# A tile's transposes asked for one projection later, with four row buffers, and staged weight blocks made on GpSimd

## The chip, the cores and the metric

The kernel runs on one core of one Trainium2 chip. The metric is the device time of one execution in microseconds (us). The kernel before was timed three times; a profiled execution, one more, gives the trace on which the reading rests. Engine names: PE is the matrix engine (PEld its weight loads), DVE the vector engine, ACT the scalar engine, POOL is GpSimd, SP is the sync engine, which here only issues transfers (DMAs).

## The reference

A transformer block in float32 with 2048 rows and 640 columns: attention in a window of 256 with 32 heads of width 20, and a gated network whose gate mixes the rows.

```
h  = x  + attention(layernorm(x), wqkv) @ wo
z  = gelu(layernorm(h) @ w_in)              # 640 -> 1728
z1, z2 = z[:, :864], layernorm(z[:, 864:])
g  = w_sp @ z2 + b_sp                       # 2048 x 2048 times 2048 x 864
out = h + (z1 * g) @ w_out                  # 864 -> 640
```

## The kernel before, in words

A tile is 128 of the 2048 rows; there are NT = 16. Products in full precision are made of pieces: a number is split into a high part (a copy on ACT, L719, into the matrix engine's rounded format) and a low part (a subtract on DVE, L713), and high x high, high x low and low x high are summed. The products of the gated network pair two tiles and use seven products of half blocks for eight (the blocks are called B11, T1, T2, B22, T3, B21, T4); sums and differences of blocks are made on DVE and sometimes POOL.

In time order the kernel runs: the dense q, k, v product and attention (to about 460 us); the output projection; the z stage (first half of w_in's columns and part of the second); the z2 stage (layer norm of the second half); the first gate; three more z2 pairs; the second gate with the last product.

**The output projection** is a loop over 16 tiles. For tile i it loads and normalises attention's output, runs 30 matmuls (L94) into a PSUM bank wo_ps, adds the residual on DVE, and forms a layer norm: squares on ACT (L1247), small steps on DVE (L1249, L1251) and POOL (L1250), then the normalised row hn(i) on ACT (L1252). The memory of hn(i) alternates between two places in the buffer m1. The function turn_h(i) transposes hn(i) on PE, five 128 x 128 blocks (L838), copies them to a buffer ho on ACT, and stores them to hn_d in DRAM by SP (L840). In the program, turn_h(i-2) stands behind projection i, and the last two tiles' turns stand in the first two steps of the z stage.

**The z stage** works on pairs of tiles, z_pair(q). It loads two tiles of hn_d into the buffer fx (L871, L872), copies and subtracts them into the operand buffer aw, and then runs eight products (L898) per pair in steps. A list `steps` holds the products; `at(n, f)` puts a piece of work f ahead of step n (a negative n is an iteration of the projection's loop, counted from its end).

**The z2 stage and the gate.** z2_pair(8..15) forms the second half of z for two tiles (L950) and normalises it, in row buffers (rows[0..3]). The gate (first_gate, then second_gate) multiplies pieces of w_sp, loaded into fx (L1036), with blocks of z2: zl and ze. The eighth group's blocks have no room at this point, so z2_pair(12) is "ahead": its seven blocks are formed in the rows on DVE, stored to z2_d (L992), and then read back one by one into the buffer `stage` (SP, L1011), split there on ACT and DVE, and stored to zp_d with high and low part (SP, L1014). They are loaded into ze once room is there (L1015). The same memory `stage` receives a piece of w_out later (L1193), also on SP. Results of the first gate are stored to g_d from the row buffers (L1099, L1100).

**What sets the order.** Up to the end of attention the order is written by hand. From the projection on, a scheduler orders each engine's instructions by its own simulation of their times; the program's order, and so `at`, only feeds it. Every engine, and SP's and POOL's queue of DMAs with it, runs its instructions in the order it got them.

Of the kernel before, what the change touches and what calls it, by code (L numbers as in the profile page):

```python
# [7 lines left out]
F32 = mybir.dt.float32  # L8
# [26 lines left out]
def block_kernel(ctx, tc, x, wqk, wv, wo, w_in, wsp, bsp, w_out, out):  # L35
# [22 lines left out]
    z2_d = dram.tile([7, P, HF], F32, name="z2_d")  # L58
# [71 lines left out]
    def m1(lo, *shape):  # L130
        return view(mem["m1"], lo, *shape)
# [629 lines left out]
    def hn(i):  # L761
        return m1((4 + i % 2) * D, D)
# [91 lines left out]
    def z_pair(q, i, j, w):  # L854
# [27 lines left out]
        at(n0 - 5, lambda: (plus(s1, a21, a22), copy(part[T1][0], s1), minus(a21, a11, a21)))  # L882
        at(n0 - 4, lambda: (minus(a11, s1, a11), minus(a12, a12, a11), copy(ah[:, 640:1152], ri[:, :512])))
# [47 lines left out]
    def z2_pair(q, i, j, k, ahead=False):  # L931
# [54 lines left out]
        if ahead:  # L986
            at(n0 + 2, lambda: (stat(0, 1), norm(0)))
            at(n0 + 4, lambda: (stat(1, 1), norm(1)))
            b11, b12, b21, b22 = blocks
# [5 lines left out]
            at(n0 + 5, lambda: (keep(B21, b21), keep(B22, b22)))  # L995
            at(n0 + 7, lambda: (minus(b11, b12, b11), minus(b12, b22, b12)))
            at(n0 + 8, lambda: (keep(T1, b11), keep(T3, b12)))
            at(n0 + 9, lambda: minus(b11, b22, b11))
            at(n0 + 10, lambda: (keep(T2, b11), minus(b21, b21, b11)))
            at(n0 + 11, lambda: keep(T4, b21))  # L1000
# [6 lines left out]
    def staged_pieces(n0, n1):  # L1007
        raw = stage.bitcast(F32)[:, 1]
# [199 lines left out]
    staged_pieces(len(steps) + 8, len(steps) + 49)  # L1208
# [15 lines left out]
    for i in range(NT):  # L1224
# [14 lines left out]
        if i > 1:  # L1239
            turn_h(i - 2)  # L1240
# [18 lines left out]
    for n in range(len(steps)):  # L1259
        run(n)  # L1260
        if n < 2:
            turn_h(NT - 2 + n)
# [43 lines left out]
```

## Time and profile before

| | us |
|---|---|
| median of three runs | 1127.86 |
| lowest, highest | 1126.88, 1131.13 |
| the profiled execution | 1126.43 |
| its span in the trace | 1124.6 |
| PE busy in the span | 1090.6 |
| DVE, ACT, POOL busy | 719.1, 576.7, 307.4 |

Rows of the trace are read as follows. A timeline row has its start and duration in us, the engine, the line, the operation, and the tiles it writes and reads; a bracket gives the time the engine stood idle ahead of it, and what ended that. A row of waits gives who waited for whom, the us in all, the number of times and the longest. A row of a stretch gives the busy time of each engine between two moments. PEclk is the clock granted to PE, 1.00 being full speed.

### The profile page before, as it was taken

The page shows a single profiled execution, that of the slowest core. Times are in us where ns is not written, and L with a number is a line of the kernel's source. Part 1 is how long each engine was busy: PE and PEld are TensorE (multiplying, and loading weights), DVE is VectorE, ACT ScalarE, POOL GpSimd, SP SyncE. Part 2 cuts the span into 40 slices and gives each one's busy share as a digit, 9 for nine tenths or more (in the row PEclk, how much of TensorE's full clock was granted, in tenths as well). Part 3 has the DMA queues.
Part 4 walks back from the last instruction along what each step waited for, and adds up shares of the span by engine and source line. Part 5 has one row for each costly group of instructions (what it writes and reads, how often), then busy time and mean ns, then how long its engine had stood idle before and what let it go on. Part 6 is the DMA issues. An engine that isn't in the chain of part 4 may idle for free.

```text
span 1124.6 us, 27720 instructions
## 1 busy us (share of the span) xinstructions
PE 1090.6 (97%) x10667; PEld 976.9 (87%) x10667; DVE 719.1 (64%) x2049; ACT 576.7 (51%) x1228; POOL 307.4 (27%) x454
## 2 busy tenths in 40 slices
PE   8999999999999999989899999999999999999998
PEld 7998877668888776879899999889989899999998
DVE  6541113889999997687376578555547884556442
ACT  4334333259999999566666567333336521222210
POOL 3114444457777778311100254000002000000000
PEclk9999999999999999999999999999999999999999
DMA  7212665656666653688564511654371563344331
GB/s 258 77 31 100 174 213 175 207 199 200 205 214 205 203 166 122 199 277 271 208 194 161 166 54 40 200 179 166 124 256 40 177 211 118 125 148 147 99 95 59
DMA packets 88036, 181.78 MB, mean 162 GB/s; under 512 B 11536, under 2 KB 49680, under 8 KB 83984
## 3 DMA queue, kind: packets, MB, share of 16 engines
q1 hardware_dynamic: 85600, 174.76, 48.2%
q10 hardware_dynamic: 2304, 5.24, 1.2%
q8 instruction: 84, 1.38, 0.5%
q14 instruction: 48, 0.39, 0.1%
HBM read 118.65 MB, written 62.51 MB: 161 GB/s over the span
## 4 chain that ended last, share of the span: by engine, by line
PE 71%; DMA 9%; DVE 7%; issue 4%; POOL 3%; ACT 3%; SPq 2%; POOLq 0%; ACTq 0%; DVEq 0%
PE g L1086 18%; PE out_ps L1125 8%; PE pv L431 6%; PE bank L403 5%; PE bank L337 5%; PE zb L950 4%; PE zx L898 3%; PE zv L898 2%; PE qk L521 2%; PE qk L523 2%; PE qk L522 2%; DMA fx<-hn_d 2%; PE zy L898 2%; POOL sg L540 2%; DMA fx<-wsp_in 1%
## 5 line engine op out<-in xcount | busy, mean ns | idle before, releaser
L406 ACT ACTIVATE pt<-bank 128x384 f32<-128x384 f32 (+2 forms) x512 | 200.3, 492 | 11.8 <-PE bank L403 8.1
L719 ACT ACTIVATE aw<-fx 128x512 fp32r<-128x512 f32 (+2 forms) x160 | 93.0, 594 | 158.9 <-PE g L1086 91.0
L1086 PE MATMUL g<-zl,aw 128*128 128x432 f32 x768 | 171.9, 359 | 1.3 <-ACT zl L719 1.2
L349 DVE CUSTOM_DVE_ANT_0 junk<-bank,strip 128x288 bf16<-128x288 f32 x392 | 157.6, 454 | 2.6 <-PE bank L337 1.1
L1086 PEld LDWEIGHTS g<-zl,aw 128*128 128x128 f32 x768 | 143.6, 188 | 8.7 <-ACT zl L719 1.9
L1086 PE MATMUL g<-ze,aw 128*128 128x432 f32 x576 | 135.8, 363 | 6.0 <-DVE row L713 4.2
L431 PE MATMUL pv<-pt,v_sb 128*32 128x192 f32 (+3 forms) x1984 | 126.5, 321 | 2.5 <-POOL pt L411 1.8
L1086 PEld LDWEIGHTS g<-ze,aw 128*128 128x128 f32 x576 | 106.3, 188 | 14.6 <-ACT aw L719 5.5
L713 DVE TENSOR_TENSOR aw<-fx,aw 128x512 fp32r<-128x512 f32 (+2 forms) x152 | 96.9, 646 | 27.7 <-ACT aw L719 26.0
L403 PE MATMUL bank<-slot 123*32 123x288 bf16 (+5 forms) x1536 | 105.9, 280 | 3.1 <-issue 2.2
L1125 PE MATMUL out_ps<-wout,y_sp 128*128 128x320 f32 (+1 forms) x630 | 96.5, 309 | 0.4 <-ACT y_sp L135 0.4
L408 POOL TENSOR_SCALAR_AFFINE_SELECT pt<-pt 128x512 f32<-128x512 f32 x128 | 82.7, 647 | 47.1 <-ACT pt L406 46.1
L950 PE MATMUL zb<-win,aw 128*128 128x432 f32 x480 | 95.5, 359 | 0.0
L1125 PEld LDWEIGHTS out_ps<-wout,y_sp 128*128 128x128 f32 (+1 forms) x630 | 94.3, 188 | 1.2 <-ACT y_sp L135 0.7
L950 PEld LDWEIGHTS zb<-win,aw 128*128 128x128 f32 x480 | 89.9, 188 | 4.9 <-DVE aw L713 0.4
L337 PE MATMUL bank<-slot 120*32 120x288 bf16 (+2 forms) x1264 | 89.0, 283 | 1.1 <-DVE mcol L349 1.0
L537 DVE TENSOR_TENSOR rest<-qk,sg 128x512 f32<-128x512 f32 x40 | 27.7, 691 | 86.2 <-ACT sg L535 82.0
L411 POOL TENSOR_SCALAR_AFFINE_SELECT pt<-pt 128x512 f32<-128x512 f32 x112 | 73.7, 658 | 0.0
L713 POOL TENSOR_TENSOR aw<-fx,aw 128x640 fp32r<-128x640 f32 x8 | 13.5, 1692 | 217.2 <-ACT aw L719 217.2
L403 PEld LDWEIGHTS <-slot 123*32 123x32 bf16 x1536 | 52.7, 96 | 18.3 <-issue 7.4
L431 PEld LDWEIGHTS pv<-pt,v_sb 128*32 128x32 f32 x1984 | 59.5, 110 | 7.5 <-POOL pt L411 3.8
L540 POOL TENSOR_TENSOR sg<-rest,sg 128x512 bf16<-128x512 f32 x40 | 46.6, 1166 | 69.2 <-ACT sg L539 63.5
(193 smaller groups left out, 2172.7 us busy)
## 6 DMA issues: line engine op xcount, KB each, us to landing
fx<-wsp_in SPq DMA_DIRECT2D x32, 512.0 KB
slot<-qk_d SPq DMA_DIRECT2D x72, 200.0 KB
qk_d<-sg SPq DMA_DIRECT2D x32, 384.0 KB
slot<-qk_d SPq DMA_DIRECT2D x72, 160.0 KB
fx<-hn_d SPq DMA_DIRECT2D x32, 320.0 KB
o_d<-ot SPq DMA_DIRECT2D x64, 128.0 KB
z_d<-row SPq DMA_DIRECT2D x16, 432.0 KB
g_d<-row SPq DMA_DIRECT2D x16, 432.0 KB
```

The source lines that it names most:

```text
L337: nc.tensor.matmul(ps[32 * j:32 * j + 32, :n], part(st, half, 120, 0, hh, q0, 32), part(st, half, 120, 1, hh, lo + skip * j, n), start=Tru ...
L349: nc.vector.tensor_tensor_reduce(out=junk[:, :n], in0=ps[:, :n], in1=keep, scale=1.0, scalar=NEG, op0=OP.add, op1=OP.max, accum_out=m_cols ...
L403: nc.tensor.matmul(ps[32 * i:32 * i + 32, b:e], part(st, half, 123, 1, hh, k0, 32), part(st, half, 123, 0, hh, kb * P + b, e - b), start=T ...
L406: nc.scalar.activation(pt[:, hh, :n], ps[:, :n], AF.Exp, scale=SCALE)
L408: nc.gpsimd.affine_select(out=pt[:, :, :P], in_=pt[:, :, :P], pattern=[[0, 4], [1, P]], base=0, channel_multiplier=-1, compare_op=OP.is_ge ...
L431: nc.tensor.matmul(ps[32 * hh:32 * hh + 32, a - 512 * c:b - 512 * c], v_sb[:, kb, v0:v0 + 32], pt[:, hh, a - kb * P:b - kb * P], start=fir ...
L713: (eng or nc.vector).tensor_tensor(out=out, in0=a, in1=b, op=op)
L719: nc.scalar.activation(out, a, AF.Copy)
L898: nc.tensor.matmul(ps, a[x], b[:, y], start=start and m + x + y == 0, stop=stop and m == n - 1 and x == 1, skip_group_check=True)
L950: nc.tensor.matmul(b[0][:, :HF], a[t][:, x, kk], win2[0][:, y, kk, h * HF:(h + 1) * HF], start=kk + x + y == 0, stop=kk == KD - 1 and x == 1)
L1086: nc.tensor.matmul(ps, w[m][x][:, k], zc[k][m][:, y], start=start and k + x + y == 0, stop=stop and k == 3 and x == 1, skip_group_check=True)
L1125: nc.tensor.matmul(ps[j][:, :HD], src[:w, a, k, :], e1["wout"][:w, b, k, j * HD:(j + 1) * HD], start=(k == 0 and a + b == 0), stop=(k == K ...
```

## The change

There are two parts. The first touches the end of the output projection: hn(i) gets four places in turn (two in m1, two more in fx, and for tiles 14 and 15 the row buffers 2 and 3), turn_h(i-3) stands behind projection i and the last three turns in the z steps 0 to 2, and the first z pairs load and prepare their tiles later (pair 0 loads at the loop's iteration 11 and pair 1 at iteration 15; their first preparations move to the loop's last three or four iterations). The second part gives the staged blocks to GpSimd: z2_pair(12) stores its two normalised rows whole, and staged_pieces loads the pieces, subtracts where a block is a difference, splits and stores, with all of it, DMAs included, on POOL; two intermediate blocks go through a scratch tensor t_d.

```diff
     def hn(i):
-        return m1((4 + i % 2) * D, D)
+        if i % 4 < 2:
+            return m1((4 + i % 2) * D, D)
+        return rows[i % 4][:, :D] if i > 11 else view(fx, (i % 4 - 2 + i // 9 * 2) * D, D)
...
     def turn_h(i):
-        if i < NT - 2:
+        if i < NT - 3:
...
-        at(max(n0 - 13, -10), load)
-        at(n0 - 7, lambda: copy(ah[:, :640], ri))
-        at(n0 - 6, lambda: lo(ah[:, :640], al[:, :640], ri))
+        at(max(n0 - 13, 4 * q - 5), load)
+        at(max(n0 - 7, -4), lambda: copy(ah[:, :640], ri))
+        at(max(n0 - 6, -3), lambda: lo(ah[:, :640], al[:, :640], ri))
...
         if ahead:
-            def keep(m, raw):
-                nc.sync.dma_start(z2_d[m], raw)
-            at(n0 + 4, lambda: keep(B11, b11))
...
-            at(n0 + 11, lambda: keep(T4, b21))
+            for t in range(2):
+                at(n0 + 4 + t, lambda t=t: nc.sync.dma_start(z2_d[t], z[t]))
...
     def staged_pieces(n0, n1):
+        hi, raw = (stage.bitcast(F32)[:, k] for k in range(2))
+        eng = nc.gpsimd
+        def piece(m, src, less=None, keep=None):
+            eng.dma_start(raw, src)
+            if less is not None:
+                eng.dma_start(hi, less)
+                minus(raw, raw, hi, eng)
+            if keep is not None:
+                eng.dma_start(keep, raw)
+            eng.tensor_copy(out=stage[:, 0], in_=raw)
+            minus(stage[:, 1], raw, hi, eng)
+            eng.dma_start(zp_d[m], stage.bitcast(F32))
+        for i, p in enumerate(((B11, b11), (T1, b12, b11, t_d[0]), (B21, b21), (T2, b22, t_d[0], t_d[1]), (B22, b22),
+                               (T3, b22, b12), (T4, b21, t_d[1]))):
+            at(n0 + 6 * i, lambda p=p: piece(*p))
...
-            n = n0 + 6 * i
-            at(n, lambda m=m: nc.sync.dma_start(raw, z2_d[m]))
-            at(n + 2, lambda: copy(stage[:, 0], raw))
-            at(n + 3, lambda: minus(stage[:, 1], raw, stage[:, 0].bitcast(F32)))
-            at(n + 4, lambda m=m: nc.sync.dma_start(zp_d[m], stage.bitcast(F32)))
...
-    staged_pieces(len(steps) + 8, len(steps) + 49)
+    staged_pieces(len(steps) + 4, len(steps) + 49)
...
-        if i > 1:
-            turn_h(i - 2)
+        if i > 2:
+            turn_h(i - 3)
...
-        if n < 2:
-            turn_h(NT - 2 + n)
+        if n < 3:
+            turn_h(NT - 3 + n)
```

The order on PE at the end of the projection and the start of the z stage, before (wo_ps15 is the last tile's projection; ht_psN, or ht_aN with ht_bN, the transposes of tile N; zv0, zx0, zy0 products of the first z pair):

```order
L94 MATMUL wo_ps15_10411<-xb1_98,xb0_97 128x320 x2
L838 MATMUL ht_ps11_10338<-ident_75,m1_8947 128x128 x5
L94 MATMUL wo_ps15_10411<-xb0_97 128x320 x2
L838 MATMUL ht_ps12_10393<-ident_75,m1_8947 128x128 x5
L838 MATMUL ht_ps13_10442<-ident_75,m1_8947 128x128 x5
L898 MATMUL zv0_10465<-zl2_9595,aw_9615 128x432 x3
L898 MATMUL zv0_10465<-zl3_9596,aw_9615 128x432 x3
L838 MATMUL ht_a14_10473<-ident_75,m1_8947 128x128 x4
L838 MATMUL ht_b14_10474<-ident_75,m1_8947 128x128
L898 MATMUL zx0_10486<-zl0_9593,aw_9615 128x432 x3
```

The same place now (lines are numbered 3 higher there, and at L95 by 1; the transposes of tile 11 stand further up, behind seven of the last projection's 30 products):

```order
L95 MATMUL wo_ps15_10404<-xb0_98 128x320 x2
L841 MATMUL ht_ps12_10435<-ident_76,m1_8948 128x128 x5
L901 MATMUL zv0_10458<-zl2_9596,aw_9616 128x432 x3
L901 MATMUL zv0_10458<-zl3_9597,aw_9616 128x432 x3
L841 MATMUL ht_a13_10466<-ident_76,m1_8948 128x128 x4
L841 MATMUL ht_b13_10467<-ident_76,m1_8948 128x128
L901 MATMUL zx0_10479<-zl0_9594,aw_9616 128x432 x3
L901 MATMUL zx0_10479<-zl1_9595,aw_9616 128x432 x3
L841 MATMUL ht_a14_10487<-ident_76,row2_9612 128x128 x4
```

Three sets of transposes stood between the last two products of the projection and the first of z; now one does, and tile 13's come after six z products.

POOL's order where the staged blocks begin, before (mvz are small steps of z2's layer norm, aw operands of the gate and of z):

```order
L976 TENSOR_TENSOR mvz11_1_11633<-mvz11_1_11633,half_78 128x1
L976 TENSOR_TENSOR mvz12_0_11692<-mvz12_0_11692,half_78 128x1
L976 TENSOR_TENSOR mvz12_1_11738<-mvz12_1_11738,half_78 128x1
L713 TENSOR_TENSOR aw_9615<-fx_9616,aw_9615 128x640 x2
L976 TENSOR_TENSOR mvz13_0_12752<-mvz13_0_12752,half_78 128x1
```

And now, the first block and the beginning of the second:

```order
L979 TENSOR_TENSOR mvz12_1_11741<-mvz12_1_11741,half_79 128x1
L1006 DMA stage_9614<-z2_d_73 128x432
L1012 CAST stage_9614<-stage_9614 128x432
L714 TENSOR_TENSOR stage_9614<-stage_9614 128x432
L1014 DMA zp_d_75<-stage_9614 128x864
L1006 DMA stage_9614<-z2_d_73 128x432
L1008 DMA stage_9614<-z2_d_73 128x432
L714 TENSOR_TENSOR stage_9614<-stage_9614 128x432
L1011 DMA t_d_74<-stage_9614 128x432
L1012 CAST stage_9614<-stage_9614 128x432
```

Where POOL had nothing to do between two z2 pairs, it now has 38 instructions, 20 of them DMAs.

SP's order in the first gate, before, from the third pair's store on (row buffers to g_d are the gate's results, fx from wsp_in the weights of a later pair, stage from w_out_in the load into the staged memory):

```order
L1014 DMA zp_d_74<-stage_9613 128x864
L1099 DMA g_d_71<-row2_9611 128x864
L1193 DMA stage_9613<-w_out_in 128x640
L1036 DMA fx_9616<-wsp_in 128x1024
L1100 DMA g_d_71<-row3_9612 128x864
L1036 DMA fx_9616<-wsp_in 128x1024
L1099 DMA g_d_71<-row0_9609 128x864
L1036 DMA fx_9616<-wsp_in 128x1024
```

Now, from two pairs later on:

```order
L1105 DMA g_d_71<-row3_9613 128x864
L1041 DMA fx_9617<-wsp_in 128x1024
L1104 DMA g_d_71<-row2_9612 128x864
L1198 DMA stage_9614<-w_out_in 128x640
L1041 DMA fx_9617<-wsp_in 128x1024
L1105 DMA g_d_71<-row1_9611 128x864
L1041 DMA fx_9617<-wsp_in 128x1024
L1104 DMA g_d_71<-row0_9610 128x864
L1020 DMA ze0_10526<-zp_d_75 128x864
```

The staged blocks' loads and stores are gone from SP's queue, and the load of w_out into their memory has moved from the third pair's store of g (the row buffer 2, 760.54 us in the trace) to the fifth's (794.33 us).

More of the change, by code (lines that the diff above doesn't have):

```diff
@@ L57, in block_kernel @@
     wo_d = dram.tile([KD, P, D], F32, name="wo_d")
-    z2_d = dram.tile([7, P, HF], F32, name="z2_d")
+    z2_d = dram.tile([2, P, FH], F32, name="z2_d")
+    t_d = dram.tile([2, P, HF], F32, name="t_d")
     zp_d = dram.tile([7, P, 2, HF], F32, name="zp_d")
@@ L877, in lo @@
             minus(l, raw, h.bitcast(F32))
[L879 to L883 removed]
+        at(max(n0 - 13, 4 * q - 5), load)
+        at(max(n0 - 7, -4), lambda: copy(ah[:, :640], ri))
+        at(max(n0 - 6, -3), lambda: lo(ah[:, :640], al[:, :640], ri))
+        at(max(n0 - 5, -3), lambda: (plus(s1, a21, a22), copy(part[T1][0], s1), minus(a21, a11, a21)))
+        at(max(n0 - 4, -3), lambda: (minus(a11, s1, a11), minus(a12, a12, a11), copy(ah[:, 640:1152], ri[:, :512])))
         at(n0 - 3, lambda: lo(*part[T1], s1))
```

8 lines of the change are left out of this document (1 added, 7 removed).

## The prediction

> **What bounds the kernel now.** I read the page's busy times first, then a table of stretches, then what TensorE waits for in the two stretches that the change touches, then the chain that ended last.
>
> ```profile
> PE 1090.6 (97%) x10667; PEld 976.9 (87%) x10667; DVE 719.1 (64%) x2049; ACT 576.7 (51%) x1228; POOL 307.4 (27%) x454
> ```
>
> TensorE is busy for 97% of the span, so a change that leaves the matmuls alone can only bring back idle time of PE. The table by stretches (start and end, length, then busy us of PE, PEld, DVE, ACT, POOL, the granted clock, the DMA share, GB/s) tells where that lies.
>
> ```profile
> 460.00:546.00 86.00, 79.11 (x549) 77.32 (x548) 61.82 (x149) 50.42 (x91) 8.66 (x14) 0.98 0.83 276
> 546.00:556.00 10.00, 6.96 (x37) 6.13 (x36) 2.02 (x10) 7.76 (x15) 1.65 (x3) 0.83 0.35 134
> 556.00:640.00 84.00, 84.00 (x433) 80.46 (x432) 51.88 (x104) 52.23 (x96) 1.60 (x1) 1.00 0.52 171
> 640.00:709.00 69.00, 69.00 (x352) 65.72 (x351) 53.68 (x103) 46.41 (x80) 33.67 (x29) 1.00 0.23 71
> 709.00:762.00 53.00, 48.40 (x240) 43.98 (x239) 30.20 (x52) 18.56 (x37) 0.00 (x0) 1.00 0.54 187
> 762.00:838.00 76.00, 74.91 (x380) 70.88 (x379) 39.13 (x63) 28.18 (x51) 0.00 (x0) 1.00 0.53 170
> ```
>
> The output projection and the step into the z stage (460 to 556) lose 86.00 - 79.11 + 10.00 - 6.96 = 9.9 us; the z and z2 products lose nothing; the first gate loses 53.00 - 48.40 = 4.6 us up to 762 and 1.1 after it. The waits of PE from 430 to 560 us, and its timeline around the end of the projection, name the first loss (time in all, times, longest; then start, duration, and in brackets the idle time before the row).
>
> ```profile
> PE ht_ps L838 <- ACT m L1252: 7.8, 5, 2.5
> PE wo_ps L94 <- DVE xb L173: 1.6, 1, 1.6
> PE ht_ps L838 <- ACT ho L719: 0.5, 1, 0.5
> ```
>
> ```profile
> 495.40 0.76 PE L838 MATMUL ht_ps<-ident,m 128*128 128x128 f32 x5 [2.38 <-ACT m L1252]
> 550.88 1.10 PE L838 MATMUL ht_ps<-ident,m 128*128 128x128 f32 x5 [2.54 <-ACT m L1252]
> 551.64 2.51 PE L898 MATMUL zv<-zl,aw 128*128 128x432 f32 x6
> 560.06 1.33 PE L898 MATMUL zx<-zl,aw 128*128 128x432 f32 x6
> ```
>
> Of the 9.9 us, 7.8 are transposes that stand on PE before ACT has written the normalised row (L1252). Idle time costs twice: six products at 551.64 take 2.51 us, and six like them at 560.06 take 1.33, so the pause is followed by 1.2 us of slow clock. The other pause has its own:
>
> ```profile
> 495.00:500.00 5.00, 4.60 (x22) 4.60 (x23) 3.52 (x10) 2.92 (x6) 1.06 (x1) 0.66 0.98 382
> 500.00:521.00 21.00, 21.00 (x148) 20.73 (x146) 18.66 (x48) 15.48 (x32) 2.31 (x4) 1.00 0.90 308
> ```
>
> A granted clock of 0.66 over 5 us is 5 x 0.34 = 1.7 us. In the 21 us after it PE is never idle, though DVE is busy for 18.66 and the DMA engines at 0.90: those two are near a limit, but are not the limit.
>
> In the gate, the waits from 709 to 762 us and the chain read as follows.
>
> ```profile
> PE g L1086 <- DVE row L713: 3.5, 3, 1.9
> PE g L1086 <- ACT aw L719: 1.1, 1, 1.1
> ```
>
> ```profile
> ACT stage L719 <- DMA stage<-z_d: 20.5, 6, 4.8
> DVE stage L713 <- ACT stage L719: 12.2, 5, 3.2
> ```
>
> ```profile
> 704.67 4.35 DMA z_d<-row
> 709.04 2.69 DMA stage<-z_d
> 712.98 2.41 DMA zp_d<-stage
> ...
> 753.85 2.40 DMA zp_d<-stage
> 756.26 2.42 DMA stage<-z_d
> 760.66 66.30 PE g L1086 x336
> ```
>
> ACT and DVE, which feed the gate, stand 20.5 and 12.2 us behind the staged blocks' loads, and PE stands 3.5 + 1.1 = 4.6 us behind them. From 760.66, when the staged work is over, PE runs 336 products without a break. So what each half of the change can win has a ceiling: about 11 to 13 us in the projection, with the clock, and 4.6 to 5.7 in the gate.
>
> **Part 1: the projection.** The program asks for turn(i-3) in place of turn(i-2), but the scheduler had already put the transposes four to five projections behind and now pulls the last ones forward: the transposes of tiles 11, 12 and 13, which stood inside and behind the last projection, become 11 inside it, 12 behind it, and 13, 14, 15 among the first z products. What makes this free is the number of buffers, four normalised rows in place of two: ACT need no longer wait for a turn before it writes the next row, and PE meets a row that has long been written. I take the whole 7.8 + 0.5 us as gone, with the 1.7 us of clock at 495: 10.0 us. The 1.6 us behind DVE xb (L173) stays. z starts at 551.64 - 10.0 = 541.6 us.
>
> What is late next: four of the added rows lie where the z stage's first tiles are to be loaded. Loads of tiles were issued (chain rows: start, duration) at
>
> ```profile
> 483.54 7.23 DMA fx<-hn_d
> 512.52 5.81 DMA fx<-hn_d
> 523.97 6.55 DMA fx<-hn_d
> ```
>
> 483 to 524 us before, well ahead. Now the load of tile 2 waits for turn 10 and that of tile 3 for turn 11, which stands behind the seventh of the last projection's 30 products. 25 products take 3.67 us, so the 23 left take 3.4, that load issues near 538, and it lands after the 5.81 to 7.23 us of the rows: at 544 to 545.
>
> ```profile
> 538.36 3.67 PE wo_ps L94 x25
> ```
>
> ACT's copy from tile 3 and DVE's subtract stand in their queues ahead of the sum and the row of tile 15 and ahead of evacuations of the first z products. PE has some 26 products of 0.196 us (1.17 for six, chain row below) and two sets of transposes in hand, about 6 us, so it runs out near 547, when the ACT and DVE work behind the load is under way.
>
> ```profile
> 554.97 1.17 PE zx L898 x6
> ```
>
> The stall lies between nothing (the load lands at 544 and the copies are quick) and 7.2 us (a whole load). I take 3.0, since the load lands ahead of 547 but three or four ACT and DVE steps of 0.6 to 0.9 us follow it; the 1.2 us of clock then stays as it is. The first part is 10.0 - 3.0 = 7.0 us faster, 3 to 10 with its bounds.
>
> SP's queue is moved too: behind the loads of tiles 0 to 3 stand loads of later tiles and win1's pieces. They come 10 to 50 us later than before, when the queue had room (DMA share 0.35 from 546, 0.52 from 556), so I cost that at nothing beyond the stall.
>
> **Part 2: the staged blocks on GpSimd.** ACT loses seven copies and DVE eleven subtracts (7 here, 4 that stood in the z2 rows):
>
> ```profile
> L719 ACT ACTIVATE stage<-stage x7: 562/564/567, 711.7 to 758.8; 128x432 fp32r<-128x432 f32 x7
> L713 DVE TENSOR_TENSOR stage<-stage x7: 596/607/610, 712.3 to 759.4; 128x432 fp32r<-128x432 f32 x7
> ```
>
> 7 x 0.564 = 3.9 us and 11 x 0.607 = 6.7 us: off the path by themselves, but with them go the waits of 20.5 and 12.2 us in those queues, and so PE's 4.6 us. Against it stands sharing between DVE and POOL:
>
> ```profile
> L713 DVE TENSOR_TENSOR aw<-fx,aw 128x512 fp32r<-128x512 f32 x3 | 2.8, 917 | 0.4 <-ACT aw L719 0.4
> ```
>
> ```profile
> L713 DVE TENSOR_TENSOR aw<-fx,aw 128x512 fp32r<-128x512 f32 x39 | 26.4, 686 | 10.5 <-ACT aw L719 10.4
> ```
>
> 917 ns in 640 to 700 us, where POOL is about half busy, against 686 in the gate, where it is not used. The z2 stretch, where this happens, still has PE busy 69.00 of 69.00 us, and DVE in the gate is busy 30.20 of 53. I leave 0.6 us for it: 4.0 us faster, from 2.5 to 5.7.
>
> POOL takes over a serial chain: per block a load, a cast, a subtract and a store, with four more loads and subtracts. The trace has no DMA issued by GpSimd and no cast there. The subtract is known:
>
> ```profile
> L713 POOL TENSOR_TENSOR row<-row,row 128x432 f32<-128x432 f32 x6 | 8.1, 1344 | 7.2 <-DVE row L713 3.4 <-ACT row L982 1.5 <-DVE zl L713 1.1
> ```
>
> 11 x 1.34 = 14.7 us; seven casts between ACT's 0.56 and 1.34, taken as 0.85: 6.0; four second loads at 0.7 us of issue each (estimate): 2.8. That is 23.5 us beside 14 transfers in series of L each. L is at least the 2.4 to 2.7 of SP's rows above; a factor of two is the far end. I take 3.2, nearest to those rows: 14 x 3.2 + 23.5 = 68 us, from 709 to 777. With L = 2.6 it ends at 769, with 5.2 at 805. The Trainium skill ("DMA: Bandwidth & Descriptors", Anatomy of one DMA, the gpsimd path) gives 2.0 us plus size over 436 GB/s, by which 216 KB take 2.5 and 432 KB 3.0 us; by it the chain would end near 771 (an estimate), and no run so far shows it.
>
> Who waits for the chain: only the load of w_out into the same stage memory, on SP, now behind the store of g that came fifth after 762.50, and behind it in the queue the wsp load that came next.
>
> ```profile
> 762.50 0.33 SPq L1193 DMA_DIRECT2D stage<-w_out_in  x1
> ...
> 794.33 0.33 SPq L1099 DMA_DIRECT2D g_d<-row  x1
> 797.58 0.33 SPq L1036 DMA_DIRECT2D fx<-wsp_in  x1
> ```
>
> In before's clock that wait becomes due at 794 and hurts from 797.6. Seen from a gate that runs earlier by 7.0 in start and 4.0 in work, the chain starts earlier by 7.0 as well, so only the 4.0 count: it must end by 793. At 777 it has 16 us to spare. The blocks themselves are wanted after 838.
>
> Sum: 7.0 + 4.0 = 11.0 us. The profiled execution took 1126.43 us (span 1124.6), 1.4 below the median of the three runs: 1115.4 on its scale, 1116.9 on the median's; I write 1117.0.
>
> **The rivals.** First, slower: GpSimd's chain outlasts its deadline and SP stands behind the w_out load, with wsp loads and stores of g behind it. It decides from 793, so from L = (793 - 709 - 23.5) / 14 = 4.3 us. PE cannot run ahead of a wsp load by more than one pair, so what is late beyond it is lost almost one to one. With L at 6.3 (POOL's issue held up behind DVE work besides the transfer, 3.7 above SP's rows) it ends at 821, 28 late: 7.0 and 4.0 won, 28 lost, 1127.9 + 17 = 1145; at L = 5.2, 12 late, about 1129. For it speaks that POOL shares something with DVE (686 to 917 ns) and is slower at each step (1344 against 607); against it that DVE is idle for over 40% of the gate. The Trainium skill ("SBUF — State Buffer", SBUF: two separate sides) states a rule that speaks for it: the shared port pair is held for a whole instruction, and a GpSimd-issued DMA of 620 ns took about 3100 beside a DVE copy. The longer DVE rows agree with sharing; whether issues suffer, no row here shows. I give this rival 0.13, of which 0.09 is slower by over 0.5%.
>
> Second, the opening of z gives most of the first gain back. If tile 3's load takes 7 us and pairs 0 and 1 are prepared behind it, now that their preparation has moved from 505 to 530 us into the opening, PE stands 7 us and more: 10.0 - 7.5 + 4.0 = 6.5, so 1121.4, and with a second pause at pair 2 about 1124. For it: the last 10 us of the projection have a DMA share still high.
>
> ```profile
> 536.00:546.00 10.00, 10.00 (x73) 9.99 (x72) 2.92 (x13) 6.64 (x12) 1.65 (x3) 1.00 0.87 314
> ```
>
> Against it: DVE has only 2.92 and ACT 6.64 us of work in these 10, so the preparations fit. Chance 0.20.
>
> Third, the projection does not get shorter by 10.0, as the pauses were hiding DVE (18.66 of 21 us busy) and the transfers (0.83 of the time over 86 us). Were DMA at 0.95 the limit, 86 us could only become 86 x 0.83 / 0.95 = 75, so it does not bind; DVE's slack does not forbid it either, but one late add costs 1 to 2 us. A gain of 5 there less 3 is 2, with the gate's 4: 1122. Chance 0.10. That the change does not do what it says is the case where rows still come late to PE, in its own right 0.04: only the gate's 4.0 is left less the stall of 3.0, near 1127.
>
> **How the numbers follow.** The forecast has 0.53; the rivals 0.13, 0.20, 0.10 and 0.04. Half a per cent, 5.6 us, is about what a measurement of this kernel can tell from no change, so faster means below 1122.2 and slower above 1133.5. Faster: all of the forecast (0.53), two thirds of the second (0.13), half of the third (0.05), a little of the first: 0.72. Slower: 0.09. Same: 0.19. The forecast's own bounds are 10.0 + 5.7 = 15.7 and 3 + 2.5 = 5.5 us, so 1112 to 1122; the low end goes to 1110 for the clock that an opening without a pause would keep (1.2), the high end to 1127, which holds the second and third rivals.
>
> **What would show it.** Right: no wait of ht_ps behind ACT m of more than 0.5 us, clock 1.00 through 495 to 500, z's first product near 541.6; one or two PE waits of together about 3 us within 10 us of it, ended by ACT or DVE that stand behind a load of hn_d; in the gate no ACT or DVE wait for stage and PE waits under 1 us; POOL's last store of zp_d near 766 to 775 by the clock of after, ahead of the w_out load. Wrong: POOL DMAs of over 4.3 us in mean, a gap of PE near 790 behind wsp loads, gaps of over 6 us at z's opening, or a projection that ends after 546.

## The result, and the profile after

The changed kernel's median is 1119.49 us (six runs, 1116.56 to 1122.58) against 1129.0 for the kernel before (six runs, 1126.88 to 1131.13). The ratio is 0.9928 with an interval of 0.9903 to 0.9953: 8.1 us less, between 5.3 and 11.0. The forecast was 11.0 less. The sum came out near and of the right sign. Of its two terms the first did not hold and the second came out larger, as the runs below show. The profiled execution took 1121.05 us (span 1119.3).

Instants of two traces can't be set against each other here: attention, which the change doesn't touch, ended at 459.6 us before and at 462.7 in this trace (457.3 in a second trace of the same kernel). So each stage is measured from its own start. Line numbers differ by a few from kernel to kernel: in the changed kernel's rows the projection's residual sum is L1249, its squares are L1252 and the normalised row is L1257 (L1244, L1247 and L1252 before). The starts are the first products of each stage; in the changed kernel these rows have them (operation, count, shortest, median and longest ns, first and last start):

```profile
L95 PE MATMUL wo_ps<-xb x220: 302/309/614, 462.7 to 549.6; 128*128 128x320 f32 x110
...
L901 PE MATMUL zv<-zl,aw x120: 352/358/467, 550.2 to 638.3; 128*128 128x432 f32 x120
```

Stretches worked out from such rows in every run that follows, in us: projection (first wo_ps to first zv), z and z2 (to the first product of the gate), gates (to the first product of the last stage) and tail (to the span's end).

| kernel | projection | z, z2 | sum of both | gates | tail |
|---|---|---|---|---|---|
| before | 92.0 | 146.3 | 238.3 | 207.6 | 219.1 |
| changed | 87.5 | 148.0 | 235.5 | 202.4 | 218.7 |
| changed, second trace | 89.0 | 147.3 | 236.3 | 202.5 | 218.7 |
| GpSimd pieces alone | 90.9 | 146.0 | 236.9 | 201.3 | 219.1 |
| projection part alone | 88.7 | 147.9 | 236.6 | 208.0 | 218.7 |
| long chain | 88.8 | 147.6 | 236.4 | 203.3 | 218.7 |
| tied load | 89.4 | 147.7 | 237.1 | 201.9 | 219.4 |
| early weights | 86.2 | 148.2 | 234.4 | 203.2 | 218.7 |
| rows 2 and 3 | 87.0 | 145.5 | 232.5 | 204.5 | 218.7 |
| rows, turn(i-2) | 88.2 | 147.4 | 235.6 | 201.4 | 219.0 |
| rows, early weights | 89.8 | 145.5 | 235.3 | 201.7 | 219.1 |
| the same, low parts on POOL | 93.1 | 145.4 | 238.5 | 207.7 | 219.2 |
| two transpose places | 87.0 | 146.4 | 233.4 | 202.1 | 218.7 |
| rows, two transpose places | 87.4 | 145.4 | 232.8 | 202.1 | 218.7 |

The gates won 5.2 us, the projection 4.5, and z and z2 lost 1.7 (5.1, 3.0 and 1.0 in the second trace). Most runs have one trace; the two of the changed kernel differ by 1.5 us in the projection and by 0.8 in the sum of both stretches, so a difference of that size between two rows of the table shows nothing. The table by stretches of the changed kernel, with the same columns as before's:

```profile
460.00:546.00 86.00, 78.72 (x582) 75.78 (x571) 61.00 (x143) 52.26 (x100) 11.38 (x18) 0.98 0.82 270
546.00:556.00 10.00, 9.26 (x62) 8.77 (x61) 5.61 (x19) 6.22 (x14) 1.10 (x2) 1.00 0.47 167
...
709.00:762.00 53.00, 53.00 (x271) 50.67 (x270) 30.25 (x45) 19.04 (x35) 17.20 (x23) 1.00 0.54 184
762.00:838.00 76.00, 74.91 (x378) 70.31 (x377) 39.36 (x61) 26.01 (x46) 14.32 (x16) 1.00 0.61 202
```

In the gate from 709 to 762 us PE is busy for all 53.00 us, where it lost 4.6. In the projection, counted from its own start to its own end, PE stands 6.7 us of the 87.5, where it stood 9.9 of the 92.0. What PE waits for from 455 to 565 us in the changed kernel tells why:

```profile
PE ht_ps L841 <- ACT ho L720: 5.6, 3, 3.1
...
PE wo_ps L95 <- DVE xb L174: 1.0, 1, 1.0
PE zx L901 <- DVE mvc L1249: 0.7, 1, 0.7
```

The 7.8 us behind ACT's normalised row are gone, as forecast; 5.6 us (4.2 in the second trace) behind ACT's evacuation of the transposes (ho), which were 0.5 before, stand in their place. The two largest of them in PE's timeline, and ACT's timeline ahead of the first:

```profile
494.69 0.71 PE L841 MATMUL ht_ps<-ident,fx 128*128 128x128 f32 x5
...
503.75 1.33 PE L841 MATMUL ht_ps<-ident,fx 128*128 128x128 f32 x5 [3.07 <-ACT ho L720]
...
521.58 0.76 PE L841 MATMUL ht_ps<-ident,fx 128*128 128x128 f32 x5 [1.83 <-ACT ho L720]
```

```profile
494.14 0.82 ACT L1252 ACTIVATE m<-xh,mvc 128x640 f32<-128x640 f32 x1
...
499.39 0.56 ACT L720 ACTIVATE zl<-wraw 128x432 fp32r<-128x432 f32 x1 [4.34 <-DMA wraw<-w_in_in]
...
503.02 0.68 ACT L720 ACTIVATE ho<-ht_ps 128x640 f32<-128x640 f32 x1
```

The transposes of 494.69 were done by 495.4, and ACT copied them out at 503.02: in its queue stood the split of w_in's next block, and that waited 4.34 us for its load. Five more ACT steps behind the split, from 499.86 on, also came ahead of the copy, so the load is only a part of its delay. All of the projection's transposes share one place in PSUM, so the next five at 503.75 had to wait for that copy.

GpSimd's chain, in POOL's timeline of the changed kernel (its first block, the first kept difference, a slow store, and its end):

```profile
710.48 0.76 POOL L1006 DMA_DIRECT2D stage<-z_d  x1 [4.76 <-DMA z_d<-row]
713.53 1.04 POOL L1012 CAST stage<-stage 128x432 fp32r<-128x432 f32 x1 [2.28 <-DMA stage<-z_d]
714.66 1.12 POOL L714 TENSOR_TENSOR stage<-stage 128x432 fp32r<-128x432 f32 x1
...
724.44 0.56 POOL L1011 DMA_DIRECT2D t_d<-stage  x1 [0.30 <-POOL stage L714]
...
730.06 1.11 POOL L714 TENSOR_TENSOR stage<-stage 128x432 fp32r<-128x432 f32 x1 [4.50 <-DMA t_d<-stage]
...
740.18 0.56 POOL L1014 DMA_DIRECT2D zp_d<-stage  x1 [0.30 <-POOL stage L714]
746.33 0.55 POOL L1006 DMA_DIRECT2D stage<-z_d  x1 [5.59 <-DMA zp_d<-stage]
...
789.23 0.56 POOL L1014 DMA_DIRECT2D zp_d<-stage  x1 [0.30 <-POOL stage L714]
```

A load took 713.53 - 710.48 = 3.05 us to use, the slowest store 6.15. And SP, which must put w_out's piece into the same memory:

```profile
790.08 0.32 SPq L1104 DMA_DIRECT2D g_d<-row  x1
792.14 0.33 SPq L1198 DMA_DIRECT2D stage<-w_out_in  x1
793.33 0.33 SPq L1041 DMA_DIRECT2D fx<-wsp_in  x1
```

The chain, started at 710.5, is over at 792.1, when SP goes on. That is 81.6 us against 68 in the forecast. The three stores of zp_d that took longest (6.15, 5.26 and 4.49 us, the others 2.9 to 3.0) are those issued within 3 us of SP's wsp loads.

### The profile page after: what moved, and what is told of

The parts are those of the page before. It is cut to its first block, busy times and chain, and to the rows that moved or that the text cites. A ratio compares the mean times of both kernels' runs of the same rounds, so it can differ in the third digit from the quotient of the medians.

```text
span 1119.3 us, 27705 instructions
## 1 busy us (share of the span) xinstructions
PE 1088.3 (97%) x10667; PEld 976.1 (87%) x10667; DVE 715.4 (64%) x2038; ACT 573.9 (51%) x1222; POOL 336.4 (30%) x492
## 4 chain that ended last, share of the span: by engine, by line
PE 59%; DMA 5%; DVE 4%; ACT 2%; issue 1%; SPq 1%; POOL 1%; DVEq 0%; ACTq 0%; POOLq 0%
PE g L1091 22%; PE out_ps L1130 8%; PE zb L953 7%; PE pv L432 5%; PE bank L338 4%; PE bank L404 4%; PE wo_ps L95 2%; PE zx L901 2%; PE zv L901 1%; PE zy L901 1%; PE yt_ps L1119 1%; DMA wraw<-w_in_in 1%; DMA fx<-w_in_in 1%; DVE zl L714 1%; DMA m<-r_d 1%
## 5 line engine op out<-in xcount | busy, mean ns | idle before, releaser
L953 PE MATMUL zb<-win,aw 128*128 128x432 f32 x480 | 95.4, 359 | 0.0
L714 DVE TENSOR_TENSOR row<-g,row 128x432 f32<-128x432 f32 x80 | 47.9, 602 | 27.9 <-PE g L1091 22.5
```

What stands on the lines that cost most here:

```text
L714: (eng or nc.vector).tensor_tensor(out=out, in0=a, in1=b, op=op)
L953: nc.tensor.matmul(b[0][:, :HF], a[t][:, x, kk], win2[0][:, y, kk, h * HF:(h + 1) * HF], start=kk + x + y == 0, stop=kk == KD - 1 and x == 1)
```

## The experiments

**GpSimd pieces alone.** The kernel before with the change's second part only.

```diff
-            at(n0 + 4, lambda: keep(B11, b11))
...
-            at(n0 + 11, lambda: keep(T4, b21))
+            for t in range(2):
+                at(n0 + 4 + t, lambda t=t: nc.sync.dma_start(z2_d[t], z[t]))
...
-    staged_pieces(len(steps) + 8, len(steps) + 49)
+    staged_pieces(len(steps) + 4, len(steps) + 49)
```

> The kernel before with the staged blocks on GpSimd, and nothing else. Theory: PE's 4.6 us of waits between 709 and 762 us go, and the chain on POOL (81.6 us in the changed kernel's trace, 710.5 to 792.1) ends about when the w_out load is due; from the first gate product (697.9 us before) to the first product of the last stage (905.5) it takes 202.4 us in place of 207.6, so 5 us less, ratio 0.9955. Rival, the chain comes just too late without the first part: 2 us less or none, a wait of PE of 2 to 4 us around 800 us. Second rival, the two parts only gain together: no change.

Measured: ratio 0.9942 (0.9921 to 0.9962), 6.5 us less (4.3 to 8.9) at a median before of 1127.77. The gates take 201.3 us in place of 207.6, and PE has no wait at all between 709 and 762 us. The theory holds, and this part gains without the other.

**The projection part alone.** The changed kernel with the staged blocks as they were, that is the kernel before with the change's first part (the buffers and turns are shown; z's later loads and preparations are in it too):

```diff
-        return m1((4 + i % 2) * D, D)
+        if i % 4 < 2:
+            return m1((4 + i % 2) * D, D)
+        return rows[i % 4][:, :D] if i > 11 else view(fx, (i % 4 - 2 + i // 9 * 2) * D, D)
...
-        if i > 1:
-            turn_h(i - 2)
+        if i > 2:
+            turn_h(i - 3)
```

> The kernel before with the four row buffers, the later turns and the later loads of the z stage, and the staged blocks as they were. Theory: projection and z opening give 4.5 us and lose 1.7 in the z stage, 2.8 us in all, ratio 0.9975; from the first projection product to the first z product 87.5 us in place of 92.0; the waits of ht_ps behind ACT m (7.8 us) are gone, those behind ACT ho are about 5. Rival, what I predicted: 7 us, ratio 0.994, hardly any wait behind ACT ho. Second rival: the opening of z gives all of it back, no change.

Measured: ratio 0.9988 (0.9969 to 1.0008), 1.4 us less, from 3.5 less to 0.9 more. Its waits of PE in the projection and in the gate:

```profile
PE ht_ps L840 <- ACT ho L719: 3.7, 3, 2.3
PE wo_ps L94 <- DVE xb L173: 2.5, 2, 1.7
```

```profile
PE g L1088 <- DVE row L713: 3.3, 3, 1.7
PE g L1088 <- ACT aw L719: 0.7, 1, 0.7
```

The gate's waits are there as before (4.0 us), and those of the projection have changed their releaser. The predicted 7 us are outside the interval. The theory's 2.8 lies in it; the second rival, no change, can't be excluded.

**A longer chain.** Each staged block stored twice.

```diff
-            eng.dma_start(zp_d[m], stage.bitcast(F32))
+            for _ in range(2):
+                eng.dma_start(zp_d[m], stage.bitcast(F32))
```

> The changed kernel with each staged block stored twice, so that POOL's chain is seven transfers longer (about 3 us each): it ends near 813 instead of 792 us. Theory (SP stands behind the w_out load into the same memory): the wsp loads behind it are late by 20 us and PE stands 12 to 20 us before 830 us, so the time is 12 to 20 us above the changed kernel, slower than before. Rival (nobody that matters waits for it, the buffered loads cover it): at most 3 us above the changed kernel.

Measured: ratio 0.9942 (0.9919 to 0.9965), the changed kernel's within the intervals; the gates take 203.3 us. SP's timeline tells that the experiment did not put the question:

```profile
787.05 0.32 SPq L1105 DMA_DIRECT2D g_d<-row  x1
793.44 0.33 SPq L1042 DMA_DIRECT2D fx<-wsp_in  x1
...
819.15 0.33 SPq L1199 DMA_DIRECT2D stage<-w_out_in  x1
```

The scheduler, which knew of the longer chain, put the w_out load 27 us later. But the wsp load that followed it in the changed kernel at 793.33 goes out at 793.44 here, with nothing ahead of it. So in the changed kernel's trace the chain's end at 792.1 cost nothing, with 1.3 us to spare (1.7 if both instants are counted from the first product of their own gate).

**A load tied to the chain.** The long chain, and the wsp loads of the first gate's last pair made to wait for the staged memory and asked for three steps later.

```diff
             for t, o in ((p, 0), (p + 8, 1024)):
+                if p == 7 and c == 0:
+                    nc.sync.dma_start(view(fx, f0 + o, 8), stage.bitcast(F32)[:, 0, :8])
...
-        at(n0 - (10 if p == 1 else 23 if alone else 11), load)
+        at(n0 - (8 if p == 7 and c == 0 else 10 if p == 1 else 23 if alone else 11), load)
```

> The kernel of the long chain with two tiny transfers on SP from the staged memory into the two halves of fx, ahead of the wsp loads of the gate's last pair, so that SP must stand there until POOL's chain is over, near 814 us, with stores of g and wsp loads queued behind; the scheduler cannot move the wait away as it did with the w_out load. Theory of the prediction (lateness of wsp loads is lost one to one): the last pair's load lands at 822 to 826 us and PE stands 8 to 14 us, so the time is 8 to 14 us above the long chain. Rival (double loads and the z2 pairs cover it): under 3 us.

Measured: ratio 0.9933 (0.9908 to 0.9959), the gates 201.9 us: nothing lost. SP's timeline, and the stretch behind it:

```profile
787.93 0.32 SPq L1107 DMA_DIRECT2D g_d<-row  x1
803.67 1.16 SPq L1043 DMA_DIRECT2D fx<-stage  x2
...
805.57 1.49 SPq L1044 DMA_DIRECT2D fx<-wsp_in  x3
```

```profile
800.00:838.00 38.00, 36.94 (x186) 34.25 (x185) 20.56 (x31) 13.47 (x24) 5.78 (x6) 1.00 0.83 291
```

SP stood from 788 to 803.7 (the tie was released by the last cast, not by the last store, so 10 us sooner than meant), three loads left at 805.6, 12 us later than the one at 793.4, and PE lost no more than elsewhere (36.94 of 38 us busy, 36.85 in the long chain). Lateness was not lost one to one where the scheduler had planned for it; this run can't tell what an unplanned one costs. Two traces below have one, that of rows 2 and 3 and that of the low parts on POOL.

**Early weights.** The second part of w_in's first half is loaded at the projection's start into memory that lies idle there.

```diff
+        raw1 = [rows[b].rearrange("p (h c) -> p h c", h=2) for b in range(2)]
+        raw2 = stage.bitcast(F32)
+        for b in range(2):
+            nc.sync.dma_start(raw1[b], src[(1 + 2 * b) * P:(2 + 2 * b) * P])
+        nc.sync.dma_start(raw2, src[4 * P:])
...
-                if k:
-                    load_win1(k, b)
...
```

> The changed kernel with the second part of w_in's first half loaded into rows 0 and 1 and into stage, which lie idle in the projection, at the projection's start instead of into the memory that the first part still holds. Theory (ACT stands up to 4.4 us behind late w_in loads with the evacuation of transposes queued behind it, and one bank holds all transposes): ACT's waits of 4.4 and 4.3 us go, PE's 5.6 us behind ACT ho shrink to under 2, the projection takes 84 us in place of 87.5, total 3 us below the changed kernel. Rival (DVE, busy 10.00 of 10 us in two stretches, or the DMA engines are the limit): within 1 us of the changed kernel, the waits turn up behind DVE xb or DVE mvc.

Measured: ratio 0.9921 (0.9894 to 0.9948). The projection falls to 86.2 us, less than hoped (84), and the total can't be told from the changed kernel's. The waits of 3.07 and 1.83 us in the middle are gone, and one of 3.20 us stands at its end, in PE's and ACT's timelines:

```profile
547.01 0.77 PE L843 MATMUL ht_ps<-ident,m 128*128 128x128 f32 x5 [3.20 <-ACT ho L720]
```

```profile
545.63 0.74 ACT L720 ACTIVATE aw<-fx 128x640 fp32r<-128x640 f32 x1 [2.17 <-DMA fx<-hn_d]
...
546.28 0.69 ACT L720 ACTIVATE ho<-ht_ps 128x640 f32<-128x640 f32 x1
```

The same queue, held up by another load: one of the z stage's opening. So the theory on the cause of the middle waits holds. PE stands 6.4 us in this projection, 6.7 in the changed kernel's: what the one load gave the next took back.

**Row buffers in rows 2 and 3 only**, and z's loads and preparations as before the change.

```diff
-        return rows[i % 4][:, :D] if i > 11 else view(fx, (i % 4 - 2 + i // 9 * 2) * D, D)
+        return rows[i % 4][:, :D]
...
-        at(max(n0 - 13, 4 * q - 5), load)
+        at(max(n0 - 13, -10), load)
...
```

> The changed kernel with the two added row buffers in rows 2 and 3 for every tile, none in fx, and the z stage's loads and preparations asked for where they stood before. Theory (part of the first half's gain is lost at the z opening, through loads that wait for turns, 0.7 + 0.5 + 0.3 us there and 148.0 us from the first z product to the gate against 146.3 before): the z stage takes 146.5 us again, 1 to 2 us below the changed kernel; the waits behind ACT ho stay at 4 to 5 us. Rival (the memory does not matter): same as the changed kernel within 1 us.

Measured: ratio 0.9933 (0.991 to 0.9957). The z and z2 stretch takes 145.5 us, 1.8 to 2.5 less than the changed kernel's two traces, and PE has no wait left in it. The run moves the rows out of fx and the loads back at once, so it doesn't separate the two. All four traces with these rows and turn(i-3) have 145.4 or 145.5; the next run, with the same rows and turn(i-2), takes 147.4, with PE waits of 1.7 us that come 11 to 31 us after z's start and not in its opening. In the total this kernel can't be told from the changed kernel. Its trace loses some 2 us in the gates (204.5 against 202.4 and 202.5): POOL's chain is 85.8 us long, SP stands 4.8 us behind it, and SP's and PE's timelines have:

```profile
789.61 0.33 SPq L1198 DMA_DIRECT2D stage<-w_out_in  x1
790.04 0.38 SPq L1041 DMA_DIRECT2D fx<-wsp_in  x1
```

```profile
795.92 0.86 PE L1091 MATMUL g<-ze,aw 128*128 128x432 f32 x3 [1.28 <-DVE row L714]
```

Counted from the gate's first product, the wsp load left at 97.6 us, at 95.1 and 95.4 in the changed kernel's two traces. The margin is thin enough for one execution to lose it: in the other traces with seven single stores the chain takes 80.4 to 83.5 us, and 87.5 in one more, below.

**The same with turn(i-2)**: the three places of the change that say 3 say 2 again.

> The kernel of the run with the rows, with turn(i-2) in place of turn(i-3), so four buffers and no later turn. Theory (the number of buffers is what matters, as the scheduler puts the turns where it likes): within 1 us of the run with the rows. Rival (the later request matters): 2 us or more above it, with waits behind ACT m back at several us.

Measured: ratio 0.9934 (0.991 to 0.9958), with rows alone 0.9933. In the total the later request does nothing that shows; four buffers do what is done. Up to the gate this trace is 3.1 us longer than that of rows alone, and its gates are 3.1 shorter, where that one's chain came late; with one trace each the stretches don't settle it. Waits behind the rows are back, 3.1 us in all, so the rival has that much right, and those behind ho are 3.4 instead of 3.9.

**Rows and early weights together.**

> The kernel of the run with the rows, and the second part of w_in's first half loaded early as in the run on the weights. Theory: with both the late loads of w_in and the late loads of the z opening out of ACT's queue, nothing holds up the evacuation; waits behind ACT ho under 1.5 us, from the first projection product to the gate 232 us (235.5 in the changed kernel, 234.4 with early weights alone), 3 us below the changed kernel. Rival (DVE, busy 10.00 of 10 us for two stretches, is the limit): waits behind DVE xb or ACT ho remain, within 1 us of the changed kernel.

Measured: ratio 0.9902 (0.9873 to 0.993); from the projection to the gate 235.3 us, not 232. ACT's waits for w_in are down to 1.1 us and PE's behind ho to 1.3, as expected. A load of hn_d still holds ACT for 4.0 us at 500, and DVE is busy throughout (start and end, then PE, PEld, DVE as above):

```profile
480.00:495.00 15.00, 12.49 (x72) 11.46 (x69) 14.94 (x31) 10.40 (x19) 1.05 (x1) 0.89 0.95 313
```

The rival's account, DVE as the next limit, fits these 15 us; PE's waits in the projection are spread over DVE xb (1.9), the rows (1.8) and ho (1.3).

**The low parts on POOL.** The last kernel, with 14 subtracts of w_in's blocks moved from DVE to POOL.

```diff
-            minus(pieces()[m][:, 1], raw[m], pieces()[m][:, 0].bitcast(F32), e)
+            minus(pieces()[m][:, 1], raw[m], pieces()[m][:, 0].bitcast(F32), low or e)
...
+                                  low=nc.gpsimd):
```

> The kernel with the rows and early weights, with the low parts of w_in's seven-block pieces made on POOL instead of DVE (14 subtracts of about 0.6 us on DVE, 1.1 to 1.35 on POOL). Theory (what is left in the projection is DVE, busy 14.94 of 15 us from 480 to 495): PE's idle time in that stretch, 2.5 us, halves, the projection takes 86 us in place of 89.8, total 2 to 4 us below the run with rows and early weights. Rival (POOL's steps in the row's layer norm come late behind the subtracts): waits of ht_ps behind ACT row or m come back with 5 us or more, total above that run.

Measured: ratio 0.9977 (0.9955 to 1.0), so some 8 us lost against the run above; the projection takes 93.1 us. The rival had the sign, but not the reason: PE waits 6.1 us behind ho, and not behind the rows. DVE's rows from 464 to 535 us, with the low parts on DVE and then on POOL:

```profile
L714 DVE TENSOR_TENSOR wraw<-wraw 128x432 f32<-128x432 f32 x4 | 2.4, 601 | 0.0
L714 DVE TENSOR_TENSOR row<-row,row 128x432 f32<-128x432 f32 x3 | 1.8, 602 | 0.0
```

```profile
L714 DVE TENSOR_TENSOR row<-row,row 128x432 f32<-128x432 f32 x3 | 4.5, 1511 | 0.0
L714 DVE TENSOR_TENSOR wraw<-wraw 128x432 f32<-128x432 f32 x4 | 4.2, 1052 | 0.0
```

The same subtract on DVE takes 1511 or 1052 ns instead of 602 beside a POOL that does subtracts. What DVE was spared it spent on longer instructions: it is busy 64.7 us in the projection, 64.0 before the move. The Trainium skill ("SBUF — State Buffer", SBUF: two separate sides) says that DVE and GpSimd share a port pair which one instruction holds to its end; 1511 is 602 and most of one POOL subtract of 1258 to 1449 ns, which agrees.

The projection is only a part of the loss. Between the two traces, 10.4 us apart, 3.3 lie in it and 6.0 in the gates. (The traced execution took 1129.27 us, near the highest of its twelve; their median is 1125.80.) The gates have the case that the tied load did not: here too the chain came late unplanned, after 87.5 us, with one load of 6.55 us in it that took 3.42 in the trace above. That the moved subtracts caused this is not shown. SP's and PE's timelines:

```profile
793.82 0.32 SPq L1107 DMA_DIRECT2D g_d<-row  x1
800.46 0.33 SPq L1201 DMA_DIRECT2D stage<-w_out_in  x1
800.89 0.38 SPq L1044 DMA_DIRECT2D fx<-wsp_in  x1
```

```profile
807.40 0.86 PE L1094 MATMUL g<-ze,aw 128*128 128x432 f32 x3 [3.43 <-DVE row L714]
```

SP stood 6.6 us, 4.6 more than in the changed kernel (2.1), and PE stood 3.43 us as the wsp load came late: it left 100.2 us after the gate's first product. With the trace of rows 2 and 3 that makes two: 2.6 us more of lateness cost PE 2.2 us more. The predicted rival exists. In the changed kernel's two traces it did not strike, by a margin of 1 to 2 us.

**Two places for transposes**, two for projections (one and three before).

```diff
-        return pools["c"].tile([P, 2, 512], F32, tag="acc", bufs=3, name=name)
+        return pools["c"].tile([P, 2, 512], F32, tag="acc", bufs=2, name=name)
...
-        return pools["c"].tile([P, 2, 512], F32, tag="aux", bufs=1, name=name)
+        return pools["c"].tile([P, 2, 512], F32, tag="aux", bufs=2, name=name)
```

> The changed kernel with two PSUM places for transposes and two for projections, in place of one and three. Theory (PE stands 5.6 us behind ACT ho only because one place holds all transposes): those waits fall under 1.5 us; if two places for projections suffice, the stretch from the first projection product to the gate falls from 235.5 to 231 us or less. Rival (ACT and DVE are late with all their work, and the evacuation is just the first to show it): the waits move to wo_ps behind DVE xh or xb, at 5 us or more, and the stretch stays within 1.5 us of 235.5 or grows.

Measured: ratio 0.9895 (0.9871 to 0.992), beside 0.9926 for the changed kernel on the same chip. Its waits of PE from 455 to 560 us:

```profile
PE wo_ps L95 <- DVE mvc L1249: 6.1, 2, 5.3
PE ht_a L841 <- DVE mvc L1249: 0.7, 1, 0.7
```

No wait behind ho is left, which fits that the single place is what let ACT's delay reach PE. But a place for projections was given up for it, and a wait of 5.3 us for a projection's place, which DVE's residual sum (L1249) frees, has come in: PE stands 6.1 us in this projection, 6.6 and 6.7 in the changed kernel's. The stretch from the projection to the gate is 233.4 us, 2.1 and 2.9 below the changed kernel's two traces and short of the 231 expected. Theory and rival each had a half.

**The changed kernel again**, beside the last two.

> The changed kernel once more beside the two others, for its stretches: 1.2 us less than before from the first projection product to the gate and 5 from there to the last stage; ratio 0.991 to 0.995 by the runs so far, against 0.990 predicted.

Measured: 0.9926 (0.9899 to 0.9953); the stretches are in the table, 2.0 and 5.1 us less than before.

**Rows and two places together.**

> The two edits that helped a stretch each, together: row buffers in rows 2 and 3 with the z stage's loads where they stood before (z stage 145.5 us to the gate with it), and two PSUM places for transposes (no waits behind ACT ho). Theory, the gains add, since they lie in different places: from the first projection product to the gate 231 to 232 us, ratio 0.987 to 0.988. Rival: they do not add, as the early preparations of z bring DVE work back into the projection; a wait behind DVE of 5 us and more in the projection, 233 to 235 us, ratio 0.990 or above.

Measured: ratio 0.9892 (0.9862 to 0.9923), from the projection to the gate 232.8 us. Compared with two places alone the gains hardly add: z and z2 keep their 145.4, and the projection stays at 87.4, with the wait of 5.3 us behind DVE in it that the rival named. It is the best ratio measured here, by no more than two places alone; both beat the kernel before, by 8.7 to 15.6 us by the wider interval, and lie below the changed kernel with overlapping intervals.

## Why the prediction was right in sum, and wrong in its terms

- **The bound and where the idle time lay**: right. From the projection to the last stage the changed kernel's two traces are 8.0 and 7.1 us shorter, and PE's idle time there is 5.8 and 6.4 us less; the tail of 219 us is the same in every trace to 0.7.
- **Part 1, "I take the whole 7.8 + 0.5 us as gone, with the 1.7 us of clock"**: this step failed. 7.8 went and 5.6 came (4.2 in the second trace), with a granted clock of 0.89 from 495 to 510 as before. The projection became 3 to 4.5 us shorter, not 10; z's first product came at 550.2 us (547.1 less this trace's later start) and not at 541.6, and a projection that ends after 546 stood among my own signs of being wrong. I had quoted the row of 0.5 behind ho as one more gain; it was the sign of the next wait. I argued from the reader's side (a row long written) and did not follow the transposes to their end: five blocks, one PSUM place, one copy by ACT, in a queue with loads ahead of it. The early weights show the loads' part (the middle waits gone), and the two places fit the single place's (waits behind ho gone, with one behind DVE in their stead). Neither run shows that PE's idle time falls once these are cured: it stays at 6.1 us and more in every projection here.
- **The opening of z, 3.0 us**: mechanism right, size too high. The load of tile 3, in the chain that ended last (start, duration):

```profile
546.53 4.58 DMA fx<-hn_d
```

It went out 3.6 us ahead of z (3.5 forecast) and landed 4.58 later. DVE waited for it, with the residual sum of the last tile behind its subtracts, and PE behind that sum:

```profile
551.13 0.95 DVE L714 TENSOR_TENSOR fx<-fx 128x256 f32<-128x256 f32 x2 [2.02 <-DMA fx<-hn_d]
552.00 0.82 DVE L1249 CUSTOM_DVE_ANT_0 xh<-wo_ps,xh 128x640 f32<-128x640 f32 x1
```

PE lost 0.7 us there, where I took 3.0; 0.5 and 0.3 more come 32 us later. The stretch is 1.0 to 1.7 longer than before.
- **Part 1 in all**: 7.0 forecast, 1.4 measured (0.9 lost to 3.5 won). The third rival, a projection limited by more than its rows and a gain of 2, was nearer in its number; what it named as the limit, DVE, came second, behind ACT's queue.
- **Part 2, 4.0 us**: 6.5 measured alone (4.3 to 8.9), 5.2 in the traces' gates. The 4.0 lies just outside that interval, which overlaps the term's own range of 2.5 to 5.7. All of the 4.6 us of waits went, and the 0.6 that I held back for sharing were not lost. DVE does feel POOL there:

```profile
L714 DVE TENSOR_TENSOR aw<-fx,aw 128x512 fp32r<-128x512 f32 x27 | 20.2, 761 | 10.0 <-ACT aw L720 9.9
```

761 ns in 712 to 790 us against 686, but DVE is busy 30.25 of 53 us there, so it has the time.
- **POOL's chain, 68 us**: 81.6. Its steps were sized well (a subtract mostly 1.12 against 1.34, a cast 0.55 to 1.04 against 0.85); the count of transfers in series was wrong, 16 and not 14, as the two kept differences must be stored before the low part overwrites them (4.50 us of waiting at 730.06). Those two took 5.6 and 2.4 us, and the fourteen others 3.6 in mean against 3.2, with stores of up to 6.15 us beside the wsp loads. The last store left at 789, not near 766 to 775, and the margin of 16 us was in truth 1.3.
- **The first rival's price**, one to one from 793: not paid where the scheduler had planned for it (12 us late cost nothing), about right where it had not, past 1 to 2 us of slack: a wsp load 2.5 us later cost 1.3, and one 5.1 later 3.4. That the changed kernel did not pay it is in part luck, as the chain was 14 us longer than I thought.
- **The rule that a GpSimd DMA is held up beside DVE work** (the Trainium skill, "SBUF — State Buffer", SBUF: two separate sides): not seen in the gate. Its figure is for a DVE copy, and DVE's work in this gate is two-input subtracts and sums, so these runs don't test it for copies. POOL's issues took 546 to 762 ns:

```profile
L1006 POOL DMA_DIRECT2D stage<-z_d x7: 546/551/762, 710.5 to 781.8; - x7
```

The two wrong terms, 5.6 too high and 2.5 too low, cancel in part, and that is luck, as neither has to do with the other: 1.4 + 6.5 = 7.9 against the 8.1 measured and the 11.0 forecast. What stays open is whether the first part gains anything at all, and what would bring the projection below 86 us: where one wait was cured another came, behind ACT's next load or behind DVE.

## What to carry to other kernels

A wait row that is small today and lies on the same buffer as the one you remove is a candidate for what comes next; follow the data past the wait to where its place becomes free again, and read what stands in that engine's queue ahead of it. Take the parts of a change apart before believing a sum: here one part gave nearly all of it. And count the transfers of a serial chain by what overwrites what, not by loads and stores alone.

## What the runs showed of the hardware

With 14 subtracts moved from a full DVE (busy 14.94 of 15 us from 480 to 495) to POOL, DVE's own subtracts of 602 ns lasted 1052 and 1511, and the projection of that trace is 3.3 us longer. In the gate, where POOL mostly waits for its transfers (busy 17.20 of 53 us), the same neighbour cost DVE's 128x512 subtract 761 - 686 = 75 ns in mean. So in these traces the cost of sharing was larger where POOL's work was denser.

A transfer issued by GpSimd took 2.4 us from issue to use at its shortest and 6.15 at its longest in the changed kernel's chain, and the chain of sixteen came out between 80.4 and 87.5 us from trace to trace.
